# Sequence product of a Fourier layer, first pass: lower parts of loaded blocks made by adding transfers, last differences moved to VectorE

## The chip, the cores and the metric

The kernel runs on one core of one Trainium2 chip. A core has a matrix engine (TensorE, in the profile PE, its weight loads PEld), three engines for elementwise work (VectorE or DVE, ScalarE or ACT, GpSimd or POOL), a queue that issues transfers (SyncE or SP) and 16 DMA engines that move the bytes. Each engine runs its own instructions strictly in the order in which the program lists them, and waits on semaphores for the others. The metric is the device time of one execution in microseconds (us); smaller is better.

## The reference

The program is four layers on a 2048 x 640 array: attention, Fourier, attention, Fourier, each added to its input after a layer norm. The change touches the Fourier layers alone:

```python
a = jnp.einsum("bsd,ed->bse", x, dft_hid_re)
b = jnp.einsum("bsd,ed->bse", x, dft_hid_im)
y = jnp.einsum("ts,bse->bte", dft_seq_re, a) - jnp.einsum("ts,bse->bte", dft_seq_im, b)
```

with x the normalized input. The kernel takes the product along the sequence (2048 x 2048 cosines and sines, times x) first and the product along the hidden dimension afterwards. All is in fp32.

## The kernel before

A matrix product in full precision is made of three on rounded operands. Every operand is split: an upper part, the value rounded to TensorE's format (fp32r), and a lower part, the value less its upper part. Then hi x hi, hi x lo and lo x hi are summed. `split` (lines 172 to 181) does this: ScalarE writes the upper part (line 174), then VectorE subtracts it from the source (line 180). In the profile line 174 and line 180 stand for every split of the program, so the tile names tell them apart: `pt` is a loaded block of the sequence matrix, `big` the activations.

The sequence product of a layer runs in four passes (`order`, lines 1219 to 1221: two halves of the output rows, and the cosine and the sine part in each). A pass takes eight steps j in each of several phases, and multiplies 128-row blocks of x with blocks of the matrix 512 columns wide. It uses a fast scheme with seven products in place of eight, so sums and differences of blocks are needed. A load brings two blocks, p and q, into a raw buffer of 128 x 1024 (line 1260, on SP's queue). `cut_to` (line 1277) forms the differences and splits what a step multiplies:

- phase a (in the first pass of a layer divided into a1 and a2): t1 = q - p; the blocks p and t1 are split. In a1 only p is, and t1, kept in its own buffer, is split in a2.
- phase b (b7 and b5 for j of 0 and 1 in the first pass, b for the rest): p becomes q - p; q and p are split.
- phase g: t1 becomes p - t1, then p becomes t1 - q; q, t1 and p are split.

The first pass (`first` in the code) differs from the others since its a1 and a2 steps run while the layer norm of the last rows is still at work: between them TensorE makes the last of the attention's output products (line 187), VectorE their statistics (lines 1086, 232 to 236, 1092), POOL the root (line 1097), ScalarE the scaling (line 1047), and ScalarE and POOL split the normalized x (lines 174 and 180, tile `big`). In the first pass VectorE makes the differences of a1 and b (lines 1303, 1311) and of the first two g steps (lines 1315, 1319). POOL makes t1 of the other g steps (line 1327), and VectorE the difference after it (line 1328).

Split blocks go into a ring of eight slots (`ring`, lines 1225, 1500 and 1237), each with an upper half c[0] and a lower half c[1]; a slot is written again once TensorE has read it. The raw buffers are seven at first and then three in turn (lines 1210, 1258, 1504); a load waits until the block before it in that buffer has been read for the last time.

`seq` (line 1368) emits one step: loads up to three steps ahead, cuts of the next step, the parts of x (`x_to`), the matmuls (line 1397), the cuts of the step after next, and after the last step of a phase the sums that go out (`gather`; line 1446 adds a sum of two accumulators). Each of the matmul groups takes the slots in the order (hi, hi), (hi, lo), (lo, hi), and the first slot of a step is that of p in a1, of q in b and in g: so the lower part of this block is read by the step's second matmul.

Of the kernel before, what the change touches and what calls it, by code (L numbers as in the profile page):

```python
# [7 lines left out]
F32 = mybir.dt.float32  # L8
# [3 lines left out]
AF = mybir.ActivationFunctionType  # L12
OP = mybir.AluOpType
# [53 lines left out]
class Net:  # L67
# [1209 lines left out]
    def cut_to(self, n):  # L1277
        nc = self.nc
        while self.n_cut <= min(n, len(self.order) - 1):
            u = self.n_cut  # L1280
            if u == self.last_a2 + 1 and self.un < self.last_a2:
                return
            self.n_cut += 1
            ph, j = self.order[u][2:]
            if ph == "b7":
                if j:
                    self.staged(u, 0, nc.vector)
                    self.staged(u, 1)
                    self.staged(u, 2)
                continue  # L1290
            t1, r = self.t1[j], self.raw_of.pop(u, None)
            if r is not None:
                p, q = r[:, :512], r[:, 512:]
            first = self.order[u][:2] == (0, 0)
            out = []

            def cut(x, out=out):
                c = self.ring.popleft()
                self.ring.append(c)
                self.split(c[0], c[1], x)  # L1300
                out.append(c)
            if ph in ("a", "a1"):
                (nc.vector if first else nc.gpsimd).tensor_tensor(out=t1, in0=q, in1=p, op=OP.subtract)  # L1303
                src = [p] + ([t1] if ph == "a" else [])
            elif ph == "a2":
                src = [t1]
            elif ph == "b5":
                self.cut_of[u] = [self.kept.pop(j)]
                continue
            elif ph == "b":  # L1310
                nc.vector.tensor_tensor(out=p, in0=q, in1=p, op=OP.subtract)
                src = [q, p]
            elif first and j < 2:
                cut(q)
                nc.vector.tensor_tensor(out=t1, in0=p, in1=t1, op=OP.subtract)
                cut(t1)

                def rest(p=p, q=q, t1=t1, cut=cut):
                    nc.vector.tensor_tensor(out=p, in0=t1, in1=q, op=OP.subtract)
                    cut(p)  # L1320
                if j == 0:
                    self.rest_g = rest
                else:
                    rest()
                src = []
            else:
                nc.gpsimd.tensor_tensor(out=t1, in0=p, in1=t1, op=OP.subtract)  # L1327
                nc.vector.tensor_tensor(out=p, in0=t1, in1=q, op=OP.subtract)  # L1328
                src = [q, t1, p]
            for x in src:  # L1330
                cut(x)
            self.cut_of[u] = out
# [525 lines left out]
```

## Time and profile before

| | |
|---|---|
| three runs | 2135.96, 2140.94, 2141.86 us; median 2140.94 |
| the profiled execution | 2136.05 us, of which the span from first to last instruction is 2134.3 |
| granted TensorE clock | 0.998 |
| matmuls on line 1397 | first pass of the first Fourier layer from 516 us, of the second from 1578.8 us |
| transfers | all issued by SP (221248 packets); none by POOL |

The profile is one execution. It gives the busy time of each engine, the transfers, a chain of waits followed back from the last instruction, and groups of instructions by line. From the trace of the same execution come the order of time on each engine (start, duration, line, output and inputs, and in brackets how long the engine had been idle before and for what it waited) and the busy time in chosen stretches. A matmul's duration in such a list overlaps that of the next; its pace is read from the starts. "pt<-c" is the load of two blocks of the sequence matrix, 512 KB.

### The profile page before, as it was taken

Reading aid. Unit: us, or ns where it says so; the run is one execution under the profiler, and the core shown is the slowest. Engines: PE = TensorE matmul, PEld = TensorE weight load, DVE = VectorE, ACT = ScalarE, POOL = GpSimd, SP = SyncE. Lnnn points to the kernel's source line nnn. Section 1 sums busy time; section 2 is a strip of 40 time slices with the busy share of each in tenths; the row PEclk is TensorE's granted clock in tenths of the full one; section 3 lists DMA queues with packets and bytes.
Section 4 is the critical chain, followed back from the end, with each engine's and each line's share of the span. In section 5 each row is a group of like instructions: output and inputs, shape, how many; then the busy total and the mean of one; then the engine's idle time right before and its main releaser. Section 6 shows DMA issues by size and latency. Waiting matters only on the chain.

```text
span 2134.3 us, 45187 instructions
## 1 busy us (share of the span) xinstructions
PE 2091.1 (98%) x16405; PEld 1740.1 (82%) x16405; DVE 1590.8 (75%) x3936; ACT 1150.6 (54%) x2511; POOL 862.4 (40%) x975
## 2 busy tenths in 40 slices
PE   8999999999999999999999999999999999999999
PEld 8987776677778888889999877767777788888899
DVE  7448888777887968777751588877778869788787
ACT  3228877776554545543431288777755645445532
POOL 2036666864432334140230466668643334241300
PEclk9999999999999999999999999999999999999999
DMA  6556667886346454767646566678754464656653
GB/s 211 165 156 204 204 198 217 238 237 196 124 123 193 138 168 140 227 204 247 210 148 184 148 201 211 202 215 244 238 182 127 121 192 125 180 161 205 231 173 121
DMA packets 221470, 395.13 MB, mean 185 GB/s; under 512 B 39232, under 2 KB 85824, under 8 KB 221248
## 3 DMA queue, kind: packets, MB, share of 16 engines
q1 hardware_dynamic: 221248, 392.26, 59.7%
q8 instruction: 129, 2.11, 0.4%
q14 instruction: 93, 0.76, 0.1%
HBM read 273.94 MB, written 117.05 MB: 183 GB/s over the span
## 4 chain that ended last, share of the span: by engine, by line
PE 81%; DVE 7%; POOL 4%; ACT 4%; DMA 3%; issue 1%; SPq 1%; ACTq 0%; POOLq 0%; DVEq 0%
PE banks L1397 28%; PE banks L187 15%; PE banks L205 13%; PE banks L693 7%; PE banks L1652 7%; PE banks L651 5%; PE banks L619 5%; POOL ou L1327 1%; DVE banks L624 1%; POOL big L180 1%; PE banks L287 1%; DMA pt<-c 1%; ACT big L1047 1%; DMA qp<-qk_d 1%; DVE qp L180 1%
## 5 line engine op out<-in xcount | busy, mean ns | idle before, releaser
L624 DVE CUSTOM_DVE_ANT_0 banks<-banks,mask 128x384 f32<-128x384 f32 (+2 forms) x1024 | 513.6, 564 | 149.5 <-PE banks L619 121.4
L662 ACT ACTIVATE pt<-banks 128x384 f32<-128x384 f32 (+2 forms) x864 | 360.2, 472 | 78.9 <-PE banks L619 39.3
L619 PE MATMUL banks<-kp,qp 60*128 60x384 f32 (+2 forms) x1024 | 336.4, 367 | 5.0 <-DVE mc L624 3.1
L651 PE MATMUL banks<-qp,kp 61*128 61x384 f32 (+2 forms) x1024 | 335.4, 363 | 4.5 <-DMA qp<-mt 3.3
L205 PE MATMUL banks<-big,wc 64*128 64x512 f32 x1920 | 336.5, 396 | 0.4 <-DVE pt L420 0.4
L619 PEld LDWEIGHTS banks<-kp,qp 60*128 60x128 f32 x1024 | 172.1, 185 | 59.3 <-DVE mc L624 44.4
L651 PEld LDWEIGHTS banks<-qp,kp 61*128 61x128 f32 x1024 | 177.0, 185 | 44.6 <-ACT pt L662 16.0
L676 POOL TENSOR_SCALAR_AFFINE_SELECT pt<-pt 128x512 f32<-128x512 f32 x216 | 138.4, 641 | 174.8 <-ACT pt L662 144.8
L205 PEld LDWEIGHTS banks<-big,wc 64*128 64x128 f32 x1920 | 196.4, 187 | 12.4 <-DVE pt L420 0.5
L1327 POOL TENSOR_TENSOR pt<-pt,pt 128x512 f32<-128x512 f32 x36 | 67.7, 1879 | 295.2 <-DMA pt<-c 127.4
L174 ACT ACTIVATE cc<-pt 128x512 fp32r<-128x512 f32 x150 | 94.0, 626 | 151.9 <-POOL pt L1303 51.7
L693 PE MATMUL banks<-pt,vq 128*32 128x128 f32 (+1 forms) x3664 | 171.5, 311 | 2.4 <-POOL pt L676 2.4
L174 ACT ACTIVATE qp<-pt 128x512 fp32r<-128x512 f32 (+1 forms) x195 | 119.8, 624 | 93.0 <-DVE pt L1328 44.0
L180 DVE TENSOR_TENSOR cc<-pt,cc 128x512 fp32r<-128x512 f32 x150 | 124.6, 841 | 51.8 <-ACT cc L174 49.6
L1397 PE MATMUL banks<-qp,big 128*128 128x512 f32 x630 | 151.1, 391 | 5.0 <-DVE qp L180 4.0
L180 DVE TENSOR_TENSOR qp<-pt,qp 128x512 fp32r<-128x512 f32 (+1 forms) x195 | 148.3, 773 | 10.1 <-ACT qp L174 7.7
L693 PEld LDWEIGHTS banks<-pt,vq 128*32 128x32 f32 x3664 | 97.9, 109 | 58.5 <-issue 17.3
L624 DVE DVE_READ_ACCUMULATOR2_ANT mc<- 128x1 f32 x1024 | 143.0, 140 | 0.0
L1397 PEld LDWEIGHTS banks<-qp,big 128*128 128x128 f32 x630 | 117.0, 188 | 31.1 <-DVE qp L180 5.7
L680 POOL TENSOR_SCALAR_AFFINE_SELECT pt<-pt 128x512 f32<-128x512 f32 x190 | 123.6, 650 | 0.0
L1397 PE MATMUL banks<-qp,xc 128*128 128x512 f32 x480 | 117.6, 390 | 1.0 <-DVE xc L180 0.8
L1397 PEld LDWEIGHTS banks<-qp,xc 128*128 128x128 f32 x480 | 89.9, 188 | 21.1 <-DVE xc L180 1.2
(232 smaller groups left out, 4532.9 us busy)
## 6 DMA issues: line engine op xcount, KB each, us to landing
pt<-c SPq DMA_DIRECT2D x188, 512.0 KB
kp<-qk_d SPq DMA_DIRECT2D x128, 160.0 KB
qp<-qk_d SPq DMA_DIRECT2D x128, 160.0 KB
kp<-u_d SPq DMA_DIRECT2D x32, 640.0 KB
o_d<-ou SPq DMA_DIRECT2D x64, 256.0 KB
x_d<-x SPq DMA_DIRECT2D x48, 320.0 KB
v_d<-pt SPq DMA_DIRECT2D x16, 768.0 KB
vq<-v_d SPq DMA_DIRECT2D x64, 192.0 KB
```

What stands on the lines that cost most here:

```text
L174: nc.scalar.activation(hi, src, AF.Copy, scale=-1.0 if neg else 1.0)
L180: (eng or nc.vector).tensor_tensor(out=lo, in0=src, in1=hi.bitcast(F32), op=OP.subtract)
L187: self.nc.tensor.matmul(p, x, y, start=n == 0, stop=n == last)
L205: self.nc.tensor.matmul(ps[a], x[r], y[r], start=half + i == 0, stop=half == 1 and i == n - 1, skip_group_check=True)
L619: nc.tensor.matmul(p, qp[quad % 2][b:b + 60, z, qb * P:(qb + 1) * P], kp[quad % 2][b:b + 60, z, k0 * P:(qb + 1) * P], start=True, stop=True)
L624: nc.vector.tensor_tensor_reduce(out=p, in0=p, in1=self.mask[:, 384 - n * P:], scale=1.0, scalar=NEG, op0=OP.add, op1=OP.max, accum_out=mc ...
L651: nc.tensor.matmul(self.banks[:, tb[e], :n * P], kp[quad % 2][b:b + 61, z, kb * P:(kb + 1) * P], qp[quad % 2][b:b + 61, z, kb * P:(kb + n) ...
L662: nc.scalar.activation(pt[quad, kb][:, 2 * z + e, :n * P], self.banks[:, tb[e], :n * P], AF.Exp, scale=SCALE)
L676: nc.gpsimd.affine_select(out=t[:, :, 0:P], in_=t[:, :, 0:P], pattern=[[0, h], [1, P]], compare_op=OP.is_ge, fill=0.0, base=0, channel_mul ...
L693: nc.tensor.matmul(p[32 * h:32 * h + 32, (c0 - qa) * P:(c1 - qa) * P], vq[:, 96 * (kb % 4) + 21 * h:96 * (kb % 4) + 21 * h + 32], t[:, h, ...
L1397: nc.tensor.matmul(self.banks[:, bk, :], p, b[q], start=start and m == 0, stop=stop and last and m == 2, skip_group_check=True)
L1652: nc.tensor.matmul(bank[to], a, b, start=start and n == 0, stop=stop and n == last, skip_group_check=True)
```

## The change

In the first pass of each Fourier layer a block that is split just as it was loaded gets its lower part in another way. ScalarE writes the negated, rounded block into the lower half of the slot (scale -1); a transfer issued by GpSimd then adds the loaded block onto it in SBUF, which leaves the block less its upper part; and ScalarE writes the upper half with a second activation. VectorE's subtraction falls away. This holds for p in a1 from j = 2 on, for q in b, and for q in all g steps. Beside it the difference t1 = p - t1 of the g steps from j = 2 on moves, in the first pass alone, from GpSimd to VectorE.

```diff
             first = self.order[u][:2] == (0, 0)
             out = []
 
-            def cut(x, out=out):
+            loaded = r is not None and first and (p if ph == "a1" and j > 1 else q if ph in "bg" else None)
+
+            def cut(x, out=out, loaded=loaded):
                 c = self.ring.popleft()
                 self.ring.append(c)
-                self.split(c[0], c[1], x)
+                if x is loaded:
+                    nc.scalar.activation(c[1], x, AF.Copy, scale=-1.0)
+                    nc.gpsimd.dma_start(c[1].bitcast(F32), x, accum_op=OP.add)
+                    nc.scalar.activation(c[0], x, AF.Copy)
+                else:
+                    self.split(c[0], c[1], x)
                 out.append(c)
...
             else:
-                nc.gpsimd.tensor_tensor(out=t1, in0=p, in1=t1, op=OP.subtract)
+                (nc.vector if first else nc.gpsimd).tensor_tensor(out=t1, in0=p, in1=t1, op=OP.subtract)
                 nc.vector.tensor_tensor(out=p, in0=t1, in1=q, op=OP.subtract)
                 src = [q, t1, p]
```

## The prediction

> **What bounds the kernel now.** First the busy shares on the page, then stretches of time restricted to the sequence product's matmuls (line 1397), then the order of time on each engine in the first of the four passes.
>
> ```profile
> PE 2091.1 (98%) x16405; PEld 1740.1 (82%) x16405; DVE 1590.8 (75%) x3936; ACT 1150.6 (54%) x2511; POOL 862.4 (40%) x975
> ...
> 572.42:603.16 30.74, 30.74 (x129) 23.70 (x130) 1.00 0.43 135
> 603.16:646.36 43.20, 40.21 (x169) 30.99 (x168) 1.00 0.39 112
> 646.36:708.00 61.64, 61.64 (x273) 51.05 (x272) 1.00 0.59 181
> ...
> 1665.40:1707.94 42.54, 40.19 (x169) 31.07 (x168) 1.00 0.38 113
> ```
>
> ```profile
> 588.83 0.98 PE L1397 MATMUL banks<-qp,rr 128*128 128x512 f32 x3
> 592.40 1.00 PE L1397 MATMUL banks<-qp,rr 128*128 128x512 f32 x3
> ...
> 603.16 2.20 PE L1397 MATMUL banks<-qp,xc 128*128 128x512 f32 x9
> 606.18 1.63 PE L1397 MATMUL banks<-qp,vq 128*128 128x512 f32 x6 [0.81 <-DVE x L1446]
> ...
> 646.36 6.28 PE L1397 MATMUL banks<-qp,big 128*128 128x512 f32 x27
> 652.48 6.28 PE L1397 MATMUL banks<-cc,big 128*128 128x512 f32 x27
> ```
>
> TensorE is 98% busy, so time can be won only where it runs below its pace. That pace is seen in the second pass: 27 matmuls from 646.36 to 652.48, 0.2267 us each. A step of phase b (15 matmuls) should take 3.40 and a step of phase g (21) 4.76. In the first pass the b steps come every 592.40 - 588.83 = 3.57, and the eight g steps take 43.20 where 168 x 0.2267 = 38.09 would do: 5.1 us lost. The second Fourier layer loses 42.54 - 38.09 = 4.45 in its g phase. This, some 9.5 us in both layers, is what the change can win in g. In phase b (572.42 to 603.16, 129 matmuls or 29.24) another 1.5 is lost.
>
> Why b is slow:
>
> ```profile
> 590.57 0.68 DVE L1311 TENSOR_TENSOR pt<-pt 128x512 f32<-128x512 f32 x1
> 591.17 0.68 DVE L180 TENSOR_TENSOR qp<-pt,qp 128x512 fp32r<-128x512 f32 x1
> 591.95 0.69 DVE L180 TENSOR_TENSOR cc<-pt,cc 128x512 fp32r<-128x512 f32 x1
> ...
> 594.16 0.68 DVE L1311 TENSOR_TENSOR pt<-pt 128x512 f32<-128x512 f32 x1
> ...
> 588.96 0.62 ACT L174 ACTIVATE qp<-pt 128x512 fp32r<-128x512 f32 x1
> 591.29 0.63 ACT L174 ACTIVATE cc<-pt 128x512 fp32r<-128x512 f32 x1 [1.71 <-DVE pt L1311]
> ```
>
> VectorE goes round in 594.16 - 590.57 = 3.59, longer than TensorE's 3.40, so TensorE follows it. The loop is difference (L1311), then ScalarE's upper part of it (591.29), then VectorE's lower part of it (591.95). The other lower part, of q, at 591.17, lies in the gap while VectorE waits for ScalarE.
>
> **The change in b.** Six subtractions of 0.60 (590.57 to 591.17 is the spacing of two such instructions) leave VectorE in each first pass. I value them at nothing: the lower part at 591.95 waits for the activation that began at 591.29, and that one waits for L1311; without the instruction at 591.17 VectorE sits idle in that gap and the round stays 3.59. What is added lies off the round: one more activation on ScalarE, which was idle 1.71 before 591.29, and one transfer issued by POOL.
>
> What can hurt is when the lower part arrives. The negated upper part starts when the upper part starts now, 588.96, and is of use 0.66 later (591.29 to 591.95). Then POOL issues and the transfer lands. No row shows an adding transfer, nor any that POOL issues. For POOL's issue I take 0.74, the mean of POOL's smallest instruction; for the transfer 3.40:
>
> ```profile
> L1097 POOL TENSOR_TENSOR rs<-rs,half 128x1 f32<-128x1 f32 x32 | 23.8, 744 | 31.8 <-DVE nb L1092 31.8
> ...
> 599.86 0.33 SPq L1260 DMA_DIRECT2D pt<-c  x1
> ...
> 603.59 1.29 POOL L1327 TENSOR_TENSOR pt<-pt,pt 128x512 f32<-128x512 f32 x1 [34.73 <-DMA pt<-c]
> ```
>
> The load issued at 599.86 freed POOL at 603.59: 3.73, less SP's issue 0.33 is 3.40. That load moves 512 KB; an addition of 256 KB to 256 KB also reads 512 KB, so this is the nearest row. Together 4.14. From below, the whole could be so short that nothing waits; from above, POOL could be held as in the row of 3.52 us quoted below (7 us together).
>
> The lower part is then there at 588.96 + 0.66 + 4.14 = 593.76. Its second matmul runs at 592.40 + 0.23 = 592.63: **1.1 us late**. TensorE waits that once, not in every step: the transfer's start hangs on VectorE's round, not on TensorE, and six rounds at 3.59 against 3.40 leave the distance as it is. The raw buffer is released later too, when the transfer has read it: load 3.73 + 0.66 + 4.14 = 8.5, under the three rounds (10.8) after which its next use comes, so the loads on SP's queue keep up.
>
> **The change in g.**
>
> ```profile
> 600.66 0.62 ACT L174 ACTIVATE qp<-pt 128x512 fp32r<-128x512 f32 x1
> 608.14 0.62 ACT L174 ACTIVATE cc<-pt 128x512 fp32r<-128x512 f32 x1
> 612.89 0.62 ACT L174 ACTIVATE rr<-pt 128x512 fp32r<-128x512 f32 x1
> ...
> 601.62 0.69 DVE L180 TENSOR_TENSOR qp<-pt,qp 128x512 fp32r<-128x512 f32 x1
> 603.61 1.82 DVE L180 TENSOR_TENSOR qp<-pt,qp 128x512 fp32r<-128x512 f32 x1 [0.70 <-ACT qp L174]
> 609.04 0.69 DVE L180 TENSOR_TENSOR cc<-pt,cc 128x512 fp32r<-128x512 f32 x1
> 613.01 1.01 DVE L180 TENSOR_TENSOR cc<-pt,cc 128x512 fp32r<-128x512 f32 x1 [0.70 <-ACT cc L174]
> ...
> 614.05 4.41 DMA pt<-c
> 618.61 3.52 POOL ou L1327
> 622.16 1.77 DVE pt L1328
> ```
>
> Here VectorE's queue is the chain: from q's lower part of step 0 (601.62) to the last lower part of step 1 (613.01 + 1.01), which frees a buffer for the load of 4.41, which feeds POOL's difference (3.52 instead of 1.29, beside VectorE), which feeds L1328 (1.77 instead of 0.68). The change takes from it: q's lower part of step 0 (0.60); the slow row 603.61, since POOL's L1327 at 603.59 is no longer beside it (1.82 - 0.61 = 1.2); q's lower part of step 1 (0.60, the row 609.04); 0.4 of the row 613.01. All of step 1 starts 1.8 earlier and that chain ends 2.8 earlier, at 611.2. From step 2 on, VectorE's extra difference (0.60) replaces q's lower part (0.60), and POOL's 3.52 and the slow L1328 go. Its load per step stays near 3.5, under TensorE's 4.76.
>
> But the lower part of q is what a g step needs in its second matmul. Step by step, with 0.66 + 4.14 = 4.80 from the start of the negation:
> - Step 0: TensorE would begin at 603.16; the negation starts at 600.66 (no earlier, since b's round is unchanged), lands 605.46, wanted at 603.39. TensorE is 2.07 late, b's 1.1 in it. It ends at 605.46 - 0.23 + 4.76 = 609.99. L1446, 1.2 + 0.6 earlier, no longer makes it wait.
> - Step 1: negation at 608.14 - 1.8 = 606.33, landed 611.13, wanted 610.22: 0.9 more. It ends at 615.66.
> - Step 2: negation about 610.5 (612.89 less 2.4), landed 615.3, wanted 615.9: in time. From here all is ahead of TensorE, and six steps of 4.76 end at 644.22.
>
> Before, g ended at 646.36: **2.1 us won**. In the second layer g took 42.54, and now 644.22 - 603.16 = 41.06: **1.5 won**. The next pass runs at full pace, so this is kept.
>
> The Trainium skill (DMA: Bandwidth & Descriptors, Anatomy of one DMA) gives a transfer issued by GpSimd as 2.0 us plus its bytes at 436 GB/s; for 256 KB that is an estimate of 2.6 us from issue to landing. No run here shows it yet. By it b waits for nothing, g ends at 642.7, and the total comes to 2135.0.
>
> **The change in a1.** In 526 to 563 the chain of waits in order of time goes round POOL and ScalarE (root, scale, cut, upper part, lower part), TensorE following 2 us behind:
>
> ```profile
> 526.50 1.01 POOL rs L1097
> ...
> 529.83 0.52 ACT cc L174
> 530.35 0.42 ACT big L174
> 530.84 1.02 POOL big L180
> ...
> 538.67 0.52 ACT cc L174
> ...
> 562.98 0.53 ACT cc L174
> ...
> 564.27 0.68 DVE pt L1268
> ...
> 536.39 0.99 POOL L1097 TENSOR_TENSOR rs<-rs,half 128x1 f32<-128x1 f32 x1 [0.26 <-DVE nb L1092]
> ...
> 539.68 1.52 POOL L180 TENSOR_TENSOR big<-big,big 128x384 fp32r<-128x384 f32 x1 [1.50 <-ACT big L174]
> ```
>
> Three of the six new negations (beside the cuts of 529.83, the next round's, and 538.67) stand in this chain: 3 x 0.52 = 1.56. POOL's three issues lie beside the second activation and the next upper part (0.52 + 0.42 = 0.94), so 0.74 costs nothing; if an issue takes longer, the excess counts three times per pass, because the lower part on POOL and the next root are queued behind it. Against that: 0.4 because VectorE, rid of two lower parts before 526, delivers the statistics sooner; the idle 0.26 at 536.39; 0.5 because POOL's 1.52 at 539.68 has no lower part of VectorE beside it any more (1.02 at 530.84). Net **+0.4 per pass**, and it reaches the end, since VectorE's L1268 at 564.27 follows the activation of 562.98. VectorE's six lower parts here are worth nothing more.
>
> **Sum.** 2 x 0.4 - 2.1 - 1.5 = -2.8 us. The durations are those of an execution of 2136.05 (span 2134.3); the three runs have the median 2140.94. Laid on the median: **2138.1**. About 0.3% (6.4 us) is what a measurement of this kernel can tell from no change.
>
> **Rivals.** Columns of this row are the stretch, its length, and the busy time of PE, PEld, DVE, ACT and POOL.
>
> ```profile
> 530.00:540.00 10.00, 9.22 (x53) 8.13 (x52) 9.58 (x26) 5.07 (x10) 5.10 (x6) 1.00 0.57 198
> ```
>
> - *POOL's issue is slow* (other side). Against VectorE's two-input instructions POOL's own subtraction took 3.52 instead of 1.29; building a transfer may be held likewise. Each us beyond 0.94 costs 3 per pass in a1 and 1 in b and g, 8 in all. It turns the gain into a loss at about 1.3 us and shows as slower from 2.1 us; at 2.2 us: -2.8 + 2 x 1.46 + 6 x 1.26 = +7.7, **2149**. For it: VectorE is busy 9.58 of 10 us there. Against: POOL's root takes 1.0 beside it (526.50, 536.39). The Trainium skill (SBUF — State Buffer, Who interferes with whom) has descriptor writing blocked only by VectorE's 2-port modes, and infers that two-input subtractions leave it alone; by that this rival falls.
> - *The transfer is quick.* If nothing waits for it, g takes 38.1: -5.1 - 4.45 + 0.8 = -8.8, **2132**. For it: source and target are both in SBUF, where the load I took as its price comes from HBM. Against: it reads two sources.
> - *It changes nothing measurable because the gain isn't kept or the transfer is near 5 us*: **2141**, in the forecast's bounds.
> - *The transfer takes 7 us or more*: the buffer's round of 3.7 + 0.7 + 7 passes 10.8 and b slows by 0.2 a step too; **2147 to 2152**.
> - That the edit misses its target can be excluded by counting: the tests hold for a1 with j of 2 to 7, b with 2 to 7 and g with 0 to 7, 20 cuts in each layer's first pass.
>
> **Chances.** Forecast and its neighbourhood (2134.5 to 2147) 0.52; quick transfer 0.26; slow issue 0.15; slow transfer 0.07. Hence faster 0.26, same 0.52, slower 0.22. The range 2131 to 2150 takes in the quick case and the slow issue of 2.2 us.
>
> **What would show it.** After: 40 adding transfers; L1327 with 12 instructions on VectorE; b's round still 3.59 with VectorE idle about 0.6 in it; TensorE waiting for a transfer at the start of g's first two steps; g near 41 us in both layers; and the distance from a1's first negation to its POOL issue and landing. A b round of 3.4 would mean that I read the round wrongly; a1 ending more than 1 us later points to POOL's issue.

## The result, and the profile after

The changed kernel takes **2156.82 us** (median of five runs, 2156.36 to 2158.58) against 2140.94 for the kernel before in as many (2135.96 to 2141.86): a ratio of **1.0084**, 95% interval 1.0071 to 1.0097. It is slower, by 18 us as the ratio has it (16 between the two medians); 2138.1 was forecast, within 2131 to 2150. The profiled execution took 2157.99 us, of which the span is 2155.9.

From the page of the changed kernel: the span, the busy times, and the queue of the new transfers (packets, MB, share of the 16 DMA engines' span).

```profile
span 2155.9 us, 45295 instructions
...
PE 2101.5 (97%) x16405; PEld 1750.3 (81%) x16405; DVE 1570.0 (73%) x3908; ACT 1173.4 (54%) x2551; POOL 862.5 (40%) x1003
...
q0 software_dynamic: 5760, 10.49, 2.8%
```

The span grew by 2155.9 - 2134.3 = 21.6 us. TensorE's busy time, for the same 16405 matmuls, grew by 2101.5 - 2091.1 = 10.4; the other 11.2 are idle time. That is one execution of each kernel, and executions of one kernel differ by up to 6 us (2135.96 to 2141.86). The two first passes by themselves (first matmul of a1 to the end of g; stretch, length, busy time of PE, PEld, DVE, ACT and POOL, granted clock, DMA share, GB/s), first before, then after, say the same:

```profile
516.57:646.36 129.79, 122.48 (x566) 98.77 (x565) 115.44 (x232) 75.20 (x148) 50.80 (x49) 1.00 0.43 134
1578.83:1707.94 129.11, 122.47 (x566) 98.86 (x565) 114.95 (x232) 75.19 (x148) 51.38 (x49) 1.00 0.42 134
...
516.91:654.82 137.91, 125.94 (x566) 102.89 (x565) 104.42 (x218) 87.28 (x168) 53.46 (x63) 0.96 0.65 170
1589.62:1729.05 139.43, 128.22 (x567) 105.05 (x566) 106.79 (x218) 86.81 (x168) 53.25 (x63) 0.94 0.62 163
```

They are 8.1 and 10.3 us longer, 18.4 together, and TensorE is busy for 3.5 and 5.8 of these, 9.2 together. So half of the loss is waiting, and half is matmuls that run slower.

The same stretches of the matmuls' line (1404 now) as before: stretch, length, PE busy, PEld busy, granted clock, DMA share, GB/s. They are phase b, phase g and the second pass of the first Fourier layer, then b and g of the second.

```profile
576.00:610.53 34.53, 32.18 (x130) 25.06 (x130) 0.95 0.70 171
610.53:654.82 44.29, 40.59 (x169) 32.44 (x168) 0.96 0.70 169
654.82:716.00 61.18, 61.18 (x271) 50.69 (x270) 1.00 0.56 169
1647.92:1685.77 37.85, 34.32 (x130) 26.99 (x131) 0.89 0.65 159
1685.77:1729.05 43.28, 40.34 (x170) 32.55 (x169) 0.96 0.65 161
```

Phase b, 30.74 before without a gap, is 34.53 and 37.85 with some 2.4 and 3.5 us of gaps; phase g, which was to fall to about 41, takes 44.29 and 43.28. In all four stretches with transfers the granted clock is below 1; in the second pass it is 1.00 again, as it was everywhere here before.

TensorE in order of time (start, duration, instruction, in brackets the idle time and what ended it):

```profile
542.57 2.81 PE L1404 MATMUL banks<-cc,big 128*128 128x512 f32 x8 [1.91 <-DMA cc<-pt]
...
587.79 0.97 PE L1404 MATMUL banks<-cc,rr 128*128 128x512 f32 x2 [2.12 <-DMA cc<-pt]
588.56 4.30 PE L1404 MATMUL banks<-cc,qp 128*128 128x512 f32 x12
...
612.54 2.11 PE L1404 MATMUL banks<-qp,xc 128*128 128x512 f32 x8 [1.63 <-DMA qp<-pt]
624.72 3.01 PE L1404 MATMUL banks<-rr,xc 128*128 128x512 f32 x8 [2.06 <-DMA rr<-pt]
```

"cc<-pt" is an adding transfer from a loaded block into a slot. In a1, in b and in two steps of g the second matmul of the step waits about 2 us for one. After the wait at 587.79 twelve matmuls take 4.30; elsewhere twelve take 12 x .2267 plus the overlap, 2.9. The granted clock there (columns as in the stretches of line 1404):

```profile
588.11:591.52 3.41, 3.41 (x9) 2.63 (x8) 0.50 0.97 238
```

The transfer's own line: issue times on GpSimd (min/median/max in ns), who waited, and the time from issue to landing.

```profile
L1304 POOL DMA_DIRECT2D qp<-pt x18: 841/878/1385, 518.5 to 1712.0; - x18
...
  PE banks L1404: 15.1, 11
...
DMA to landing us min/median/max: 3.2/4.4/7.9
```

TensorE waited for a transfer eleven times, 15.1 us in all. The median landing, 4.4, is near the 4.14 of the prediction. The spread is not in it.

VectorE in a b step, and two rows of ScalarE and VectorE at the start of g:

```profile
590.56 0.69 DVE L1318 TENSOR_TENSOR pt<-pt 128x512 f32<-128x512 f32 x1
591.94 0.69 DVE L180 TENSOR_TENSOR qp<-pt,qp 128x512 fp32r<-128x512 f32 x1 [0.70 <-ACT qp L174]
594.15 0.69 DVE L1318 TENSOR_TENSOR pt<-pt 128x512 f32<-128x512 f32 x1
...
608.69 1.28 ACT L1471 ACTIVATE kp<-banks 128x512 f32<-128x512 f32 x2 [2.13 <-PE banks L1404]
611.87 0.69 DVE L180 TENSOR_TENSOR qp<-pt,qp 128x512 fp32r<-128x512 f32 x1 [2.58 <-ACT qp L174]
```

VectorE's round is still 594.15 - 590.56 = 3.59, with .70 idle where q's lower part was. At 608.69 a late TensorE holds ScalarE: the copies of b's results stand in its queue ahead of g's cuts, and VectorE waits 2.58 for those. A late step hands its lateness on.

Last the chain of waits, in order of time (start, us, what), in a1 and around the change from b to g:

```profile
524.85 7.38 DMA qp<-pt
532.37 4.85 DMA pt<-c
537.24 0.64 ACT cc L1303
...
597.15 6.63 DMA cc<-pt
603.85 4.40 DMA pt<-c
```

In both places a load (pt<-c) begins only when a transfer has landed: the transfer is now the last reader of the raw buffer, and the next load of it waits for that. At 537.24 ScalarE starts a cut late for this reason. The chain goes through one transfer of about 7 us and the load behind it, both times.

### The profile page after: what moved, and what is told of

Read it like the earlier page. It is cut to its first block, busy times and chain, and to the rows that moved or that the text cites. A ratio compares the mean times of both kernels' runs of the same rounds, so it can differ in the third digit from the quotient of the medians.

```text
span 2155.9 us, 45295 instructions
## 1 busy us (share of the span) xinstructions
PE 2101.5 (97%) x16405; PEld 1750.3 (81%) x16405; DVE 1570.0 (73%) x3908; ACT 1173.4 (54%) x2551; POOL 862.5 (40%) x1003
## 3 DMA queue, kind: packets, MB, share of 16 engines
q8 instruction: 129, 2.11, 0.4%
## 4 chain that ended last, share of the span: by engine, by line
PE 80%; DMA 6%; DVE 5%; POOL 4%; ACT 3%; issue 2%; SPq 1%; POOLq 0%; ACTq 0%; DVEq 0%
PE banks L1404 29%; PE banks L187 15%; PE banks L205 12%; PE banks L693 7%; PE banks L1659 6%; PE banks L651 4%; PE banks L619 4%; DMA rr<-r_d 2%; POOL big L180 1%; DMA pt<-c 1%; DMA qp<-qk_d 1%; DVE banks L624 1%; PE banks L287 1%; ACT big L1047 1%; DMA rr<-pt 1%
## 5 line engine op out<-in xcount | busy, mean ns | idle before, releaser
L651 PEld LDWEIGHTS banks<-qp,kp 61*128 61x128 f32 x1024 | 176.8, 185 | 42.4 <-ACT pt L662 15.1
L174 ACT ACTIVATE cc<-pt 128x512 fp32r<-128x512 f32 x134 | 84.0, 628 | 144.7 <-POOL pt L1310 52.0
L180 DVE TENSOR_TENSOR qp<-pt,qp 128x512 fp32r<-128x512 f32 (+1 forms) x177 | 137.2, 788 | 25.8 <-ACT qp L174 23.6
L174 ACT ACTIVATE qp<-pt 128x512 fp32r<-128x512 f32 (+1 forms) x177 | 108.8, 625 | 80.0 <-DVE pt L1335 37.0
L180 DVE TENSOR_TENSOR cc<-pt,cc 128x512 fp32r<-128x512 f32 x134 | 106.2, 803 | 57.8 <-ACT cc L174 56.2
L1334 POOL TENSOR_TENSOR pt<-pt,pt 128x512 f32<-128x512 f32 x30 | 46.9, 1563 | 207.4 <-ACT rr L174 82.6
```

Source lines behind the costliest of these rows:

```text
L174: nc.scalar.activation(hi, src, AF.Copy, scale=-1.0 if neg else 1.0)
L180: (eng or nc.vector).tensor_tensor(out=lo, in0=src, in1=hi.bitcast(F32), op=OP.subtract)
L651: nc.tensor.matmul(self.banks[:, tb[e], :n * P], kp[quad % 2][b:b + 61, z, kb * P:(kb + 1) * P], qp[quad % 2][b:b + 61, z, kb * P:(kb + n) ...
```

## The experiments

The theory after this look, called A in the expectations: the transfers land too late for a step's second matmul, not once but wherever a landing is slow; the wait, and a lower clock after it, are the loss. Rivals: the moved difference crowds VectorE (D), and GpSimd's issue or the traffic costs the time wherever the result is read (T). Each experiment was timed in five rounds against the kernel before on the same chip; the kernel before had medians of 2138.0 to 2138.8 there, so go by the ratios, not by the differences to 2140.9. For each its ratio, and the length of its stretches in the first / second layer: a from the first matmul of a1 to the first of b, b and g as above.

| kernel | median us | ratio to before (95%) | a | b | g |
|---|---|---|---|---|---|
| before | 2140.9 | | 55.85 / 55.82 | 30.74 / 30.75 | 43.20 / 42.54 |
| changed | 2156.8 | 1.0084 (1.0071 to 1.0097) | 59.09 / 58.30 | 34.53 / 37.85 | 44.29 / 43.28 |
| 1 difference moved alone | 2138.3 | 1.0001 (.9990 to 1.0012) | 55.92 / 55.91 | 30.78 / 30.82 | 43.20 / 41.57 |
| 2 transfers alone | 2154.8 | 1.0082 (1.0066 to 1.0099) | 58.90 / 57.97 | 39.98 / 38.90 | 41.89 / 44.39 |
| 3 no transfer | 2134.4 | .9974 (.9964 to .9983) | 55.78 / 55.78 | 31.19 / 30.75 | 40.01 / 40.10 |
| 4 late use | 2141.9 | 1.0016 (1.0005 to 1.0027) | 58.26 / 58.34 | 34.26 / 34.39 | 39.59 / 39.57 |
| 5 transfers in a1 | 2142.6 | 1.0019 (1.0009 to 1.0028) | 59.48 / 57.54 | 31.07 / 30.81 | 41.56 / 43.15 |
| 6 transfers in b | 2142.7 | 1.0012 (1.0001 to 1.0023) | 55.86 / 55.87 | 34.52 / 35.73 | 39.88 / 39.93 |
| 7 transfers in g | 2144.1 | 1.0030 (1.0017 to 1.0042) | 55.82 / 55.82 | 30.78 / 30.80 | 46.06 / 45.97 |
| 8 plain copy | 2141.5 | 1.0013 (1.0005 to 1.0022) | 55.82 / 56.30 | 33.00 / 32.53 | 41.76 / 41.84 |
| 9 GpSimd addition | 2166.5 | 1.0127 (1.0108 to 1.0147) | 59.15 / 59.12 | 37.12 / 37.06 | 46.59 / 46.64 |
| 10 GpSimd split | 2166.3 | 1.0131 (1.0115 to 1.0148) | 59.12 / 60.66 | 37.11 / 37.07 | 46.38 / 46.38 |
| 11 half loads | 2143.8 | 1.0025 (1.0013 to 1.0037) | 58.80 / 57.24 | 32.42 / 32.88 | 41.13 / 40.70 |
| 12 late use, not in b | 2140.0 | 1.0002 (.9992 to 1.0013) | 59.62 / 57.38 | 30.81 / 31.22 | 40.43 / 40.28 |
| 13 filled waits | 2145.2 | 1.0030 (1.0019 to 1.0040) | 55.84 / 55.80 | 30.74 / 30.78 | 43.91 / 44.90 |
| 14 late use in g alone | 2135.0 | .9989 (.9978 to 1.0000) | 55.84 / 55.82 | 30.78 / 30.77 | 40.25 / 40.26 |
| 15 its order alone | 2138.5 | 1.0003 (.9991 to 1.0015) | 55.87 / 55.86 | 30.79 / 30.76 | 41.77 / 41.79 |
| 16 as 14, beside 15 | 2135.9 | .9974 (.9962 to .9985) | 55.85 / 55.83 | 30.78 / 30.79 | 40.31 / 40.26 |

### 1 and 2: the two parts of the change

The first is the kernel before with this line alone changed; the second the changed kernel with it changed back.

```diff
-                nc.gpsimd.tensor_tensor(out=t1, in0=p, in1=t1, op=OP.subtract)
+                (nc.vector if first else nc.gpsimd).tensor_tensor(out=t1, in0=p, in1=t1, op=OP.subtract)
```

> The kernel before, with one part of the change alone: in the first pass's g steps the difference t1 = p - t1 runs on VectorE instead of GpSimd; every split stays as it was. Theory A (the adding transfers land late, and each late landing is a wait of TensorE): the slower time has nothing to do with this part, so it is at or below the kernel before, 2 to 6 us faster (2135 to 2139 against 2140.9), and TensorE's waits in g of the first pass shrink. Rival D (the moved difference crowds VectorE and is what costs): 5 to 15 us slower than the kernel before, near 2150.

> The changed kernel with the g difference put back on GpSimd; the lower parts of the loaded blocks are still made by negated copy and adding transfer. Theory A: as slow as the changed kernel or slower, 2156 to 2163. Rival D: most of the loss is gone, 2140 to 2147.

The moved difference costs nothing and, against what A hoped, wins nothing either (1.0001). The transfers alone cost what the whole change costs (1.0082). Rival D falls.

### 3: no transfer

```diff
-                    nc.gpsimd.dma_start(c[1].bitcast(F32), x, accum_op=OP.add)
```

> The changed kernel without the adding transfer: the lower part of a loaded block in the first pass is the negated upper part alone, so the addition of the block is left out of the computation. All other instructions stay. Theory A: TensorE's second matmul waits for ScalarE's copy alone, the long waits of the first pass go, and the time is below the kernel before, 2131 to 2138. Rival D or any theory in which the copies on ScalarE or the order on VectorE cost the time: it stays above 2150.

The loss turns into a gain: .9974, or 5.6 us (the kernel leaves the addition out of the computation, so only its time counts). Everything else of the change is still there, the 40 negated copies too; so the transfers are all of the loss. The stretches show the size of what could have been won: a and b are as long as before to .5, and g is 3.2 and 2.4 shorter. VectorE's relief is worth something in g alone, 5.6 us in all.

### 4: use the result later

In a1, b and g of the first pass the matmuls that read a transfer's result come last in their step.

```diff
-                for m, (p, q) in enumerate(((hi, 0), (hi, 1), (lo, 0))):
+                for m, (p, q) in enumerate(((hi, 0), (lo, 0), (hi, 1)) if late else ((hi, 0), (hi, 1), (lo, 0))):
...
+                    if late and m == 2 and b is c[0]:
+                        held.append(one)
...
+        for f in held:
+            f()
```

> The changed kernel with all its transfers, but in the first pass each step's matmuls that read the lower part made by a transfer come last in the step: in a1 and g after all the matmuls with the upper part or other blocks, in b after those of m7. Same matmuls, same count. A transfer may then land 1.4 us (a1, six matmuls later) to 5 us (b, g: 12 to 18 matmuls later) after the upper part without a wait. Theory A (lateness at the second matmul): most of the loss goes, 2133 to 2143. Rival T (GpSimd's issue of .88 us each, or the traffic of the transfers beside the loads, costs the time wherever the result is read): it stays at 2150 to 2157.

All 40 transfers, and only 3.4 us (ratio 1.0016) of 18 left. It was the time at which the result is read, and rival T falls, but for its issue in a1 (below). Phase g is even shorter than without transfers. Two remainders: b still waits for transfers (.68, 1.27 and 1.06 us in the first layer, although 12 matmuls lie in between), and a stays 2.4 and 2.5 longer though TensorE waits for no transfer there.

For the second remainder the trace of this run has the answer in the first layer. First the granted clock near the start of a1 (all engines, as in the first passes above); then two pieces of the chain of waits (start, us, what), and the same two in run 12, which has this order in a1 too:

```profile
524.14:527.55 3.41, 3.41 (x13) 3.12 (x13) 1.90 (x2) 1.77 (x4) 3.10 (x3) 0.50 0.45 80
```

```profile
522.72 2.60 PE banks L1406 x8
525.32 2.84 PE banks L187 x12
```

```profile
520.79 2.11 PE banks L1406 x8
522.90 1.77 PE banks L187 x12
```

With half the clock these two pieces are 1.56 longer together (5.44 in place of 3.88). GpSimd's issue adds most of the rest: from the start of a negation to the end of GpSimd's lower part behind it there are 2.03 us without one before (529.83 to 531.86), 2.56 with the plain copy of run 8 (534.70 to 537.26) and 2.81 here (543.10 to 545.91). The negation itself is .53 of that, and with plain copies, .53 and all, a is as long as before in the first layer (55.82); the .25 more of the adding issue, three times, is .75. Together 2.3 of the 2.4, an account from the trace that no run of its own tests.

### 5, 6 and 7: one phase at a time

```diff
-            loaded = r is not None and first and (p if ph == "a1" and j > 1 else q if ph in "bg" else None)
+            loaded = r is not None and first and (p if ph == "a1" and j > 1 else None)
```

and with `q if ph == "b"` and `q if ph == "g"` in the same place.

> The changed kernel with adding transfers in the a1 steps alone; in b and g the lower parts are made by subtraction on VectorE as before; the last difference stays on VectorE. Theory A (lateness at the second matmul, phase by phase): the a stretch of the changed kernel grew by 3.1 and 1.9 us, so 3 to 7 us slower than the kernel before, 2141 to 2145. Rival G (the loss is a result of all three phases together, by the traffic or by GpSimd being filled): each phase alone is within 2 us of the kernel before.

> The same with adding transfers in the b steps alone. Theory A: the b stretch of the changed kernel grew by 3.8 and 7.1 us, the largest part, so 7 to 12 us slower than the kernel before, 2145 to 2150. Rival G: within 2 us of the kernel before.

> The same with adding transfers in the g steps alone. Theory A: the g stretch of the changed kernel grew by 1.1 and .7 us, so 0 to 3 us slower than the kernel before, 2138 to 2141; if the lateness of g0 there was only handed on from b, up to 2 us faster. Rival G: within 2 us too, so this run tells only the sum: by theory A the three phases alone add up to about 15 to 20 us, by G to less than 6.

Each phase costs by itself: +.19%, +.12% and +.30%. The sum, .61% or 13 us, is nearer to A's 15 to 20 than to rival G's 6, but it falls short of the 18 of all three, by about what the three intervals leave open. My shares of it were off: g alone is the dearest, b alone the cheapest, and both missed their intervals (2144.1 for 2138 to 2141, 2142.7 for 2145 to 2150). In the run of b alone most of what b loses is won back in g (39.9 in place of 43.2 and 42.5). In g alone TensorE waits 1.59, 1.29 and 2.62 us in the first three steps, the same in both layers to .06.

### 8: the adding taken out of the transfer

```diff
-                    nc.gpsimd.dma_start(c[1].bitcast(F32), x, accum_op=OP.add)
+                    nc.gpsimd.dma_start(c[1].bitcast(F32), x)
```

> The changed kernel with each adding transfer turned into a plain copy of the block, from the same queue and of the same size: the addition is left out of the computation. It asks whether the adding is what makes a transfer late. If it is the adding (it reads the target too): issue to landing falls from 4.4 us to 3.4 us or less and the time to 2135 to 2145. If it is the start of a transfer on this queue and its share of the transfer engines: landing stays within .4 us of 4.4 and the time at 2150 to 2158.

The queue's row on the page of this run, then issue and landing of its transfers:

```profile
q0 software_dynamic: 3200, 10.49, 1.3%
```

```profile
L1304 POOL DMA_DIRECT2D qp<-pt x18: 536/546/747, 518.2 to 1694.7; - x18
...
DMA to landing us min/median/max: 2.3/3.3/6.5
```

The same bytes take 80 packets in place of 144 each, 1.3% of the engines' time in place of 2.8, .55 us of issue in place of .88, and land 1.1 us sooner in the median. Most of the loss goes (1.0013). So adding makes a transfer about twice as heavy for the DMA engines.

### 9 and 10: the same work by a GpSimd instruction

```diff
-                    nc.gpsimd.dma_start(c[1].bitcast(F32), x, accum_op=OP.add)
+                    nc.gpsimd.tensor_tensor(out=c[1], in0=x, in1=c[1].bitcast(F32), op=OP.add)
```

and, for the second, `self.split(c[0], c[1], x, eng=nc.gpsimd)` in place of the three instructions.

> The changed kernel with each adding transfer replaced by the same addition as one GpSimd instruction on the same tiles; the negated copy and its place stay. Such an instruction of 128x512 took 1.28 to 1.9 us on GpSimd before the change, against .88 of issue and 3.2 to 7.9 to landing for the transfer. Theory A (the landing is too late, the removal from VectorE is right): 2133 to 2140, no wait of TensorE over 1 us in the three stretches that is not in the kernel before. Rival D2 (any way of making the lower part off VectorE is late, since ScalarE's copy must come first): 2146 or more.

> The lower parts of the same blocks made on GpSimd by the plain split (upper part copied by ScalarE, then block minus upper part on GpSimd), without the negated copy; last differences on VectorE. One ScalarE copy of .63 us less for each of the 40 blocks than with the addition. Theory A: 2132 to 2139, at or below the run with the GpSimd addition. Rival: GpSimd and VectorE hold each other up when both run 128x512 operations, the chains on VectorE get longer, 2140 or more.

Both expectations of A missed: 2166, slower than the change itself. The time is that of rival D2, but not its reason: an addition is there after 1.3 to 1.8 us, and TensorE waits for one only once in each layer, .52. What happens is on VectorE, as the rival of the second run has it. In order of time, first with the GpSimd addition, then the changed kernel at the same place of a step:

```profile
585.03 1.36 POOL L1304 TENSOR_TENSOR rr<-pt,rr 128x512 fp32r<-128x512 f32 x1 [2.60 <-ACT rr L1303]
585.15 1.52 DVE L1187 TENSOR_TENSOR big<-big 128x256 f32<-128x256 f32 x1
```

```profile
589.76 0.42 DVE L1187 TENSOR_TENSOR big<-big 128x256 f32<-128x256 f32 x1
589.96 0.88 POOL L1304 DMA_DIRECT2D qp<-pt  x1 [2.68 <-ACT qp L1303]
```

VectorE's L1187, .42 us long, lasts until the GpSimd instruction is over: 1.10 more, in VectorE's round. b's steps then come every 4.69 (583.96, 588.65, 593.34) in place of 3.59. The issue of a transfer beside the same instruction lengthens nothing. It happens in five steps of b in each layer, 5.5 of the 6.4 us lost there; the loss in a and g isn't traced to it. Lateness isn't the only way to lose here; A explains the change and not these two.

### 11: half the loads

```diff
-            self.nc.sync.dma_start(r, self.a["c"][sb, part, j][:, lo:lo + 1024])
+            h = 512 if not sb + part and ph in "bg" else 0
+            self.nc.sync.dma_start(r[:, h:], self.a["c"][sb, part, j][:, lo + h:lo + 1024])
```

> The changed kernel with the loads of the first pass's b and g steps cut to the half that the transfer reads (256 KB in place of 512 KB); the other half is left out of the computation and keeps old data. All transfers stay. Contention theory (a transfer that runs beside a load lands at 6 to 8 us, one alone at 3.2 to 4): the landings of b and g fall to 5 us or less, the median to 4, and the time to 2141 to 2150. Rival (the slow landings come from the transfer's own queue or from its adding): the long landings of 6 to 8 us stay and the time is 2152 or more.

From issue to landing in phase b of the first layer, first with half loads, then in the changed kernel:

```profile
DMA to landing us min/median/max: 3.6/4.1/4.7
```

```profile
DMA to landing us min/median/max: 3.3/4.7/7.2
```

The long landings of b go; in g the maximum falls from 7.8 to 6.3, and in a1, where the loads are whole, it stays (7.2 after 7.4). Thirteen of the 18 us go with them. My bound of 5 us in g was too sharp, and so were the two ranges. By the issue times in the trace of the changed kernel, **the fourteen transfers with a load issued within .75 us of their own issue landed after 5.3 to 7.9 us, the other 26, but for one of 6.1, after 3.2 to 5.4**. The theory that a load beside it makes a transfer late holds. Smaller loads also arrive sooner, so not all of the gain need be the transfers'.

### 12: late use without b

The kernel of 4 with transfers in a1 and g alone.

> Transfers in a1 and g alone, with the matmuls that read their results last in the step; b's lower parts on VectorE as before; last differences on VectorE. The run with late use in all three phases was 3.4 us slower than the kernel before, and its waits on transfers were in b alone (.68, 1.27 and 1.06 us in the first of the two layers). Theory A: these go, 2133 to 2139. Rival (the transfers cost something wherever they are, by traffic or by the copies added): 2140 to 2143.

1.0002: A's interval of 2133 to 2139 is missed by 1 us, the rival's is touched. b and g are as hoped; a is 3.8 and 1.6 longer than before. With the changed kernel, 2, 4, 5 and 11 this makes six with adding transfers in a1, and in all of them a takes 57.2 to 59.6; without them, or with plain copies, 55.8 to 56.3 (the two with GpSimd instructions aside). In a1 a transfer doesn't pay in either order. Here, unlike in 4, the chain of waits in a1 goes through a load of 5.51 us (from 531.83), so the reason in 4 needn't be that of this run.

### 13: do the waits lower the clock?

The kernel of 7; the first matmul of g's first three steps is issued 4, 4 and 8 times more, ahead of the one that waits.

```diff
+                more = (4, 4, 8)[j] if not sb + part and ph == "g" and j < 3 and name == "m1" and i == 0 else 0
-                for m, (p, q) in enumerate(((hi, 0), (hi, 1), (lo, 0))):
-                    nc.tensor.matmul(self.banks[:, bk, :], p, b[q], start=start and m == 0,
+                for m, (p, q) in enumerate(((hi, 0),) * more + ((hi, 0), (hi, 1), (lo, 0)), -more):
+                    nc.tensor.matmul(self.banks[:, bk, :], p, b[q], start=start and m <= 0,
```

> The kernel with transfers in g alone, whose three waits of TensorE on a transfer were the same in both layers (1.6, 1.3 and 2.6 us), and in which eight matmuls behind the third wait took 3.33 us in place of 2.11. Here the first matmul of each of these three steps is issued 4, 4 and 8 more times (.9, .9 and 1.8 us at .227 each) ahead of the one that waits, so that part of the wait is filled with work; the product that it adds once more is added to one sum of the computation. Clock theory (the waits let the granted clock fall, and what follows is slower): the matmuls behind g's third step are back at .227 each and the time is 1 to 4 us below the 2144.1 of that kernel although 32 matmuls are added. Rival (the slower matmuls have another cause): the eight behind the third wait still take 3 us or more, and the time is 2144 or more.

Windows of 30 us around g's start in both layers, and the eight matmuls of the third step; first the kernel of 7, then this one:

```profile
600.00:630.00 30.00, 24.50 (x98) 19.10 (x97) 0.94 0.67 161
1669.00:1699.00 30.00, 24.64 (x99) 19.24 (x98) 0.94 0.65 156
```

```profile
617.40 3.33 PE L1404 MATMUL banks<-rr,xc 128*128 128x512 f32 x8 [2.62 <-DMA rr<-pt]
```

```profile
600.00:630.00 30.00, 28.71 (x123) 22.57 (x122) 1.00 0.66 161
1669.00:1699.00 30.00, 27.39 (x119) 21.91 (x118) 1.00 0.68 167
```

```profile
620.37 2.11 PE L1405 MATMUL banks<-rr,xc 128*128 128x512 f32 x8 [0.22 <-DMA rr<-pt]
```

With the same transfers and the same DMA share the clock is granted in full and the eight take 2.11 again. The g stretches are 2.2 and 1.1 us shorter although each holds 16 matmuls (3.6 us) more. So in g the slower matmuls come from the waits, not from the traffic. Not every such group of waits has this effect. In the run of b alone TensorE waits 1.08, 2.39 and 1.03 us within 16 us of the second layer, and the clock stays whole:

```profile
1640.00:1670.00 30.00, 25.14 (x106) 19.21 (x105) 1.00 0.70 167
```

And in run 1, which has no transfer, the clock is .50 from 617.43 to 620.84, behind waits of 1.27 us at most. What decides it the runs don't show. The time of the whole kernel doesn't show what 13 gained in g: 2145.2 against 2144.1, the same ratio of 1.0030. Three us in the stretches are about what the two intervals hide, but the 1 to 4 us expected of the time were not seen.

### 14, 15 and 16: what remains worth having

14 and 16 are the kernel of 4 with transfers and late use in g alone; 15 is the same order of matmuls with `loaded = None`, so that VectorE makes every lower part.

> Transfers in g alone, with the matmuls that read their results last in each g step; a1 and b split on VectorE as before, last differences on VectorE. The best that the findings so far suggest. Theory A: the waits on transfers in g go and VectorE has one instruction of .69 less in each of g's steps: 2134 to 2138, up to 4 us below the kernel before. Rival (what VectorE is relieved of in g has no worth once the difference is on it too): 2138 to 2141.

> The order of the matmuls of the run with late use in g alone (those that read the loaded block's lower part last in each g step), and no transfer anywhere: all lower parts on VectorE as before, last differences on VectorE. It asks what made that run's g stretch 3.0 and 2.3 us shorter than that of the kernel before. If the transfers did (VectorE has one instruction of .69 less in each g step): this one stays within 1.5 us of the kernel with the difference alone moved, 2137 to 2141, and its g stretches take 41.5 to 43.2 us. If the order alone did: 2133 to 2137, g stretches of 40 to 40.5 us.

> The same kernel as the run with late use in g alone, on the chip of the run beside it, so that the two can be compared: 2133 to 2138, g stretches of 40.3 us in both layers. Rival: its lead over the kernel before (ratio .9989, interval up to 1.0000) was chance, and it is at 1.000 or above.

From the second of the two equal kernels: phase b, nearly, and phase g of the first layer, then the landings.

```profile
573.00:603.30 30.30, 30.30 (x129) 23.38 (x129) 1.00 0.43 133
603.26:643.57 40.31, 39.14 (x169) 31.18 (x168) 1.00 0.75 181
```

```profile
DMA to landing us min/median/max: 3.4/4.1/7.7
```

The landings are as slow as ever, up to 7.7 us, and TensorE waits for none of them. This kernel beats the kernel before and 15: .9974 (.9962 to .9985) beside 15, and .9989 with an interval that reaches 1.0000 the first time; 2.4 to 5.6 us below the kernel before by the two ratios. The order alone gives 1.0003, as expected if the transfers are what wins; the 2.2 us by which its g stretches are shorter don't show in its time, and its interval could hide them. Of the 2.9 and 2.3 us by which g is shorter, the order with the moved difference has 1.4 and .8, the transfers 1.5 in each layer.

## Why the prediction was wrong

**Where it held.** VectorE's round in b stayed 3.59 with .70 idle, so the relief there is worth nothing (3: b 31.19 and 30.75). So it is in a1 (3: a 55.78 in both). GpSimd's issue took .88 for the .74 estimated, well under the 1.3 from which the rival of a slow issue would decide, so that rival falls. But that an issue under .94 costs nothing was wrong: it begins .35 after the negation's end, and in 4 each of three issues made GpSimd .25 later (.75 a pass). TensorE did wait for transfers where g begins.

**The step that failed** is the one on lateness: "TensorE waits that once, not in every step: the transfer's start hangs on VectorE's round, not on TensorE, and six rounds at 3.59 against 3.40 leave the distance as it is", with 4.14 us for every transfer. The size was near the median (4.4), but the sum needed the spread. Transfers issued beside a load land after 5.3 to 7.9 us, the others mostly after 3.2 to 5.4 (11), so a slow one is a new wait of up to 2 us: b grew by 3.8 and 7.1 in place of 1.1. For g I had 2.07 and .9 and "in time" from step 2 on; with transfers in g alone the waits were 1.59, 1.29 and 2.62, the largest in the step that I had called safe.

**"The loads on SP's queue keep up"** failed with it. I compared 8.5 with 10.8 in b, at the 4.14, and never asked the question in a1. The chain of waits after goes through a transfer of 7.38 and a load of 4.85 behind it there. Load and transfer hold each other up: the transfer is late because a load runs beside it, and the next load is late because the transfer reads its buffer.

**The price of a1** was the wrong question: I counted issues and activations (+.4 a pass) and not the landings, though TensorE followed the chain by only 2 us. The stretch came out 3.2 and 2.5 longer. Late use doesn't cure it (4 and 12), so TensorE's own waits are only a part. The load behind the transfer is seen in the changed kernel's chain; in 4 it was, by the trace, half the clock for 3.41 us and GpSimd's issues. How the 3.8 and 1.6 us of run 12 divide stays open.

**The clock** was not in the sum at all. The slower matmuls are about half of the loss (9.2 of 18.4 in the first passes), and 13 shows for g that they follow from the waits; for a and b that is taken over from there, not shown.

**The gain in g** was overrated too. I gave 5.1 and 4.45 us as what could be won, less the lateness; with no transfer to wait for, 3.2 and 2.4 were (3). The quick-transfer rival's 2132 was thus out of reach: 2134.4, a ratio of .9974, is what an instant transfer gives.

Nearest came the rival with 7 chances in 100, "the transfer takes 7 us or more", 2147 to 2152. Its landings are real, but its price was a steady .2 a step in b; the waits come in single lumps, in three phases, with the clock behind them. The 19 us between forecast and result are therefore: waits counted once that occur wherever a landing is slow, a load queue that I took to be free, and a clock that I left out. How many of the 19 each of the three took, no run separates.

## What to carry to other kernels

Don't price a transfer that replaces an instruction by its median alone: ask for its slowest landing beside the loads that run with it, where its result is first read, and who waits for the buffer that it reads. If work is taken off an engine, first test with the new work simply left out: here that run showed that two of three phases had nothing to give. Where a result can be used at the end of a step rather than at its start, landings up to 7.7 us cost nothing, and a losing change became one that wins 2.4 to 5.6 us.

## What the runs showed of the hardware

- **An adding transfer within SBUF weighs twice a plain one**: 144 packets against 80 for 256 KB, 2.8% against 1.3% of the DMA engines' time for 40 of them, 4.4 against 3.3 us to landing in the median. The estimate of 2.6 us from the Trainium skill (DMA: Bandwidth & Descriptors, Anatomy of one DMA) is under both; the fastest plain copy took 2.3, the fastest addition 3.2.
- **A GpSimd instruction that has begun stops a VectorE instruction until it is over**: 1.52 us for .42 in run 9, where L1187 subtracts two operands in SBUF and began .12 later than the addition; beside the issue of a transfer the same instruction takes .42. The Trainium skill has VectorE instructions with two SBUF inputs contend with GpSimd's reads and infers that writing a transfer's descriptors leaves them alone (SBUF — State Buffer, Who interferes with whom); the trace agrees with both. I had not asked it of my own alternative, GpSimd in place of the transfer.
- **Three waits of 1.6, 1.3 and 2.6 us within 16 us lowered TensorE's granted clock** to .94 over 30 us (7, both layers); filled to .7, .4 and .2 they left it at 1.00, and so did a wait of 2.0 behind one of .6 in the second layer of the same run (13). Waits of 1.1, 2.4 and 1.0 within 16 us left it at 1.00 too (6), so their size alone doesn't decide. The Trainium skill has the clock halved when TensorE's recent activity falls (TensorE: Matmul & The Clock Gate, Part 1: The HAM clock gate). The trace agrees as to the half: .50 for 3.41 us from 588.11 in the changed kernel, and from 617.95 in run 7.
